# The last expert place of a fused state-space scan and hash-routed MoE kernel: separate PSUM banks, a last product in two pieces, GpSimd's drain moved ahead of six scatters

## Chip, cores, metric

The kernel runs on one core of one Trainium2 chip. The metric is the device time of one execution in microseconds, the median of several runs. TensorE is called PE, VectorE DVE, ScalarE ACT, GpSimd POOL and SyncE SP, as the profile names them.

## What is computed

Two layers, one after the other, all in float32. The first is a chunked state-space scan (Mamba-2 SSD) for 4 batches, 8 heads and 768 positions. Its output is laid out as 3072 tokens of 256 values. The second sends each token to one of 8 experts by its id and applies a two-layer MLP with 256, 1024 and 256 features:

```python
expert_idx = token_ids * np.int64(2654435761) % np.int64(E)
for e in range(E):
    mask = expert_idx == e
    xe = x[mask]
    h = np.maximum(xe @ w1[e], 0.0)
    out[mask] = h @ w2[e]
```

The change lies in the last part of the second layer.

## The kernel before, in words

The kernel first runs the scan and writes its tokens to DRAM, and beside it works out for every token a slot: the tokens of one expert lie next to each other. The experts take 8 "places" p = 0 to 7, sorted by their number of tokens; place p has two halves of `HALF[p]` slots (202 down to 184). `xT` holds the slots' vectors with features on partitions; 25 tiles of 128 slots cover all slots, and the halves' borders don't fall on the tiles' borders. Place 7 has its halves at slots 2816 to 2999 and 3000 to 3183. The tiles 22, 23 and 24 are its own: tile 22 lies in the first half, tile 23 holds the end of the first half and the first 72 slots of the second, and tile 24 the last 112.

Each product of a 2 by 2 block matrix (halves of features by halves of slots) is done with 7 block products in place of 8 (Strassen's scheme in Winograd's form): sums of weight blocks (`sums_w`, on POOL, tiles s1 and s2), sums of operand blocks (`sums_x`, `sums_h`, on DVE, tiles t1 and t2), 7 products on PE and sums of the products on the way out of PSUM. `up` (L898 is its matmul) makes the first layer, `down` (L943) the second. One product of `down` is 4 matmuls of a 128x128 weight block with up to 202 columns; the trace shows each float32 matmul as two, so 8 passes a product.

The products are numbered: `down(p, 1)` leaves p1 (copied by ACT, L950), 6 leaves u2 = product + p1 (DVE, L955), 2 adds to 1 in PSUM and is the block o(0, 0) of the output (ACT, L952), 7 adds to 6 in PSUM and leaves u3 (DVE, L960), 4 adds to the same bank and gives o(1, 0) (DVE, L964), 5 leaves z in PSUM, o(1, 1) = z + u3 (DVE, L966), and 3 adds to z's bank and gives o(0, 1) = bank + u2 (DVE, L962). In o(i, j), i is the half of the features and j the half of the slots. The outputs overwrite `xT`.

`put(k)` turns tile k back (two PE transposes, L970, into one PSUM bank, then one copy to `o_sb`, L975 on ACT or L973 on DVE), and `scatter` sends its 128 rows to their tokens in the output with an indirect DMA that POOL issues (L979). `o_sb` has 4 buffers.

PE, DVE, ACT and POOL run their instructions in the order of the program text (the schedule is written by hand). `step(p)` interleaves `up(p)` with `down(p - 1)`. After `step(7)` only `down(7)` is left, which I call the last place: the sums of place 7's operand (`sums_h`, L872, L875, L877 and L879 in this order), then the products in the order 1, 6, 2, 7, 4, 5, 3, with banks given by `banks=(4, 5, 0)`: 1 and 2 in bank 4, 6, 7 and 4 in bank 5, 5 and 3 in bank 0. The last product of place 6 uses bank 4 too. The tiles of place 6 (19, 20, 21) are put after the products 1, 6 and 2, one each, all through bank 7; then POOL gets a drain instruction (L1111). Tile 22 is put ahead of the last product, the tiles 23 and 24 after it. Behind this stands a loop for experts with more tokens than their slots, which runs zero times with this input, and then the end of the program, where every engine waits for all DMAs and for each other (its instructions stand under L1122 and L1194).

Of the kernel before, what the change touches and what calls it, by code (L numbers as in the profile page):

```python
# [25 lines left out]
def kernel(  # L26
# [900 lines left out]

    dsts = {p: {} for p in range(E)}

    def down(p, what, banks=None):  # L930
        n, st = HALF[p], dsts[p]
        banks = banks or (DN[p % 2], DN[1 - p % 2], DN[p % 2])
        bank = banks[1 if what in (6, 7, 4) else 2 if what in (5, 3) else 0]
        w, s, t = w2s[p], s2[p], t2[p]
        A = lambda i, k: (lambda q: w[:, k * Q4 + q, i * P:(i + 1) * P])
        Sm = lambda i: (lambda q: s[:, i, q])
        hq = lambda k: (lambda q: hx[p][:, k, q, 0:n])
        tt = lambda i: (lambda q: t[:, i, q, 0:n])
        lhs, rhs = {1: (A(0, 0), lambda q: h11[p][:, q, 0:n]), 2: (A(0, 1), hq(1)), 3: (Sm(3), hq(2)),
                    4: (A(1, 1), tt(3)), 5: (Sm(0), tt(0)), 6: (Sm(1), tt(1)), 7: (Sm(2), tt(2))}[what]  # L940
        first = what in (1, 6, 5)
        for q in range(Q4):
            pe.matmul(out=ps[:, bank, 0:n], lhsT=lhs(q), rhs=rhs(q), start=(first and q == 0), stop=True,  # L943
                      skip_group_check=True)
        src = ps[:, bank, 0:n]
        o = lambda i, j: xT[:, i, slots(p, j)]
        dwork = lambda name: mwork.tile([P, N0], F32, name=name, bufs=1)[:, 0:n]
        if what == 1:
            st["p1"] = dwork("dp1")
            act.activation(st["p1"], src, AF.Copy)  # L950
        elif what == 2:
            act.activation(o(0, 0), src, AF.Copy)  # L952
        elif what == 6:
            st["u2"] = dwork("du2")
            dve.tensor_tensor(out=st["u2"], in0=src, in1=st["p1"], op=OP.add)  # L955
        elif what == 5:
            st["z"] = src
        elif what == 7:
            st["u3"] = dwork("du3")
            dve.tensor_tensor(out=st["u3"], in0=src, in1=st["p1"], op=OP.add)  # L960
        elif what == 3:
            dve.tensor_tensor(out=o(0, 1), in0=src, in1=st["u2"], op=OP.add)  # L962
        else:
            dve.tensor_tensor(out=o(1, 0), in0=src, in1=st["p1"], op=OP.add)  # L964
        if what in (5, 7) and "z" in st and "u3" in st:
            dve.tensor_tensor(out=o(1, 1), in0=st["z"], in1=st["u3"], op=OP.add)  # L966

# [66 lines left out]
    def step(p):  # L1034
# [12 lines left out]
        for r in range(R):  # L1047
# [22 lines left out]
                sums_x(*xs_.pop(0))  # L1070
            if p == 1 and r == 4:
                pool_e.tensor_copy(out=space, in_=t2[0][:, 3, 0, 0:1])
            if downs:
                down(p - 1, downs[r])
                if downs[r] == 4 and p + 1 < E:
# [17 lines left out]
        step(p)  # L1093

    puts = [k for k in outs if done_at[k] == E - 2]
    for i in range(4):
        sums_h(E - 1, i)
    own = [k for k in outs if done_at[k] == E - 1]
    half = [k for k in own if (k + 1) * P <= base[E - 1, 1]]
    sent = []  # L1100
    for r, w in enumerate((1, 6, 2, 7, 4, 5, 3)):
        if w == 3:
            sent = [put(k, 1 + i) for i, k in enumerate(half)]
        down(E - 1, w, banks=(4, 5, 0))
        if puts:
            scatter(*put(puts.pop(0)))
        if r == 3:
            for k in puts:
                scatter(*put(k))
            puts = []  # L1110
            pool_e.drain()  # L1111
    for o in sent:
        scatter(*o)
    for i, k in enumerate(k for k in own if k not in half):
        scatter(*put(k, (2, 3)[i % 2], eng=(act, dve)[i % 2]))

    _, rn = nc.values_load_multi_w_load_instructions(
        nov_i[0:1, 0:1], min_val=0, max_val=NCH + E,
# [80 lines left out]
```

## Time and profile before

| | |
|---|---|
| median of 3 runs | 241.43 us (239.32 to 243.09) |
| the profiled execution's own time | 242.91 us |
| its span, first to last instruction | 240.9 us |
| PE busy | 219.1 us (91%), 2264 matmuls |
| DVE busy | 175.7 us (73%) |
| POOL busy | 175.1 us (73%) |
| ACT busy | 92.0 us (38%) |

The span is what the trace covers; the profiled execution takes 2.0 us beyond it. A busy PE is counted with modelled ends of its matmuls, so the spacing from one matmul to the next tells more than the busy time. In a timeline a row gives start, length, engine, line, operation, tiles, and in brackets how long the engine had been idle before and what it waited for.

### The profile page before, as it was taken

Reading aid. Unit: us, or ns where it says so; the run is one execution under the profiler, and the core shown is the slowest. Engines: PE = TensorE matmul, PEld = TensorE weight load, DVE = VectorE, ACT = ScalarE, POOL = GpSimd, SP = SyncE. Lnnn points to the kernel's source line nnn. Section 1 sums busy time; section 2 is a strip of 40 time slices with the busy share of each in tenths; the row PEclk is TensorE's granted clock in tenths of the full one; section 3 lists DMA queues with packets and bytes.
Section 4 is the critical chain, followed back from the end, with each engine's and each line's share of the span. In section 5 each row is a group of like instructions: output and inputs, shape, how many; then the busy total and the mean of one; then the engine's idle time right before and its main releaser. Section 6 shows DMA issues by size and latency. Waiting matters only on the chain.

```text
span 240.9 us, 5848 instructions
## 1 busy us (share of the span) xinstructions
PE 219.1 (91%) x2264; PEld 201.2 (84%) x2264; DVE 175.7 (73%) x309; ACT 92.0 (38%) x192; POOL 175.1 (73%) x223
## 2 busy tenths in 40 slices
PE   7979898997859899999999999999999999999880
PEld 2668776875758699998989999999999899998770
DVE  6888979675614779899998976788678389556520
ACT  5866855934245533113033314234303422411210
POOL 8748599913535368589979988999998998980513
PEclk9999999999979999999999999999999999999995
DMA  7999899994878597019118318407107004310101
GB/s 96 160 198 136 171 187 194 171 263 148 221 179 294 186 324 215 27 51 306 61 44 272 122 44 264 174 23 220 44 0 218 28 23 134 113 61 0 46 22 63
DMA packets 52833, 33.14 MB, mean 138 GB/s; under 512 B 29708, under 2 KB 47140, under 8 KB 52806
## 3 DMA queue, kind: packets, MB, share of 16 engines
q1 hardware_dynamic: 48258, 25.74, 44.5%
q0 software_dynamic: 2400, 6.43, 8.2%
q10 hardware_dynamic: 2148, 0.60, 1.0%
q8 instruction: 18, 0.29, 0.5%
q14 instruction: 9, 0.07, 0.1%
HBM read 26.47 MB, written 6.42 MB: 137 GB/s over the span
## 4 chain that ended last, share of the span: by engine, by line
PE 43%; POOL 18%; DVE 15%; DMA 12%; issue 6%; ACT 4%; another core or an unknown queue 0%; POOLq 0%; DVEq 0%; ACTq 0%
PE ps L898 16%; DMA out_dram<-o_sb,idx_out 12%; POOL s L770 10%; PE ps L943 8%; POOL out_dram L979 4%; PE ps L370 4%; PE ps L311 3%; PE ps L153 3%; POOL xg L623 3%; DVE t L863 2%; DVE m L317 2%; PE ps L383 2%; PE ps L265 2%; DVE t L872 2%; DVE t L875 2%
## 5 line engine op out<-in xcount | busy, mean ns | idle before, releaser
L623 POOL DMA_INDIRECT xg<-y_tokens,idx_in x25 | 28.8, 1151 | 21.7 <-DVE m L317 8.2
L979 POOL DMA_INDIRECT out_dram<-o_sb,idx_out x25 | 28.8, 1151 | 18.7 <-ACT o_sb L975 9.1
L898 PE MATMUL ps<-t,s 128*128 128x202 f32 (+7 forms) x192 | 37.3, 329 | 1.2 <-ACT h L908 0.6
L770 POOL TENSOR_TENSOR s<-w 128x512 f32<-128x512 f32 x26 | 33.4, 1284 | 5.1 <-DMA w<-in_moe_w_dram 4.8
L943 PE MATMUL ps<-t,s 128*128 128x202 f32 (+7 forms) x192 | 35.3, 326 | 0.2 <-DVE t L875 0.2
L898 PEld LDWEIGHTS ps<-t,s 128*128 128x128 f32 x192 | 31.3, 189 | 2.5 <-DVE u L913 1.5
L943 PEld LDWEIGHTS ps<-t,s 128*128 128x128 f32 x192 | 31.8, 189 | 0.4 <-issue 0.4
L898 PE MATMUL ps<-xT,w 128*128 128x202 f32 (+7 forms) x128 | 26.8, 342 | 4.3 <-ACT p L904 4.1
L898 PEld LDWEIGHTS ps<-xT,w 128*128 128x128 f32 x128 | 21.6, 198 | 5.8 <-ACT p L904 5.0
L926 ACT ACTIVATE hx<-hx 128x404 f32<-128x404 f32 (+7 forms) x16 | 8.2, 524 | 32.9 <-DVE hx L925 32.7
L317 DVE COPY_PREDICATED m<-cmask,ps 128x1024 f32<-128x1024 int32 x12 | 15.2, 1310 | 4.4 <-ACT y_sb L393 3.9
L770 POOL TENSOR_TENSOR s<-w,s 128x512 f32<-128x512 f32 x13 | 17.9, 1380 | 0.5
L770 POOL TENSOR_TENSOR s<-s,w 128x512 f32<-128x512 f32 x13 | 17.8, 1372 | 0.5
L975 ACT ACTIVATE o_sb<-ps 128x256 f32<-128x256 f32 x24 | 9.2, 382 | 19.1 <-PE ps L970 10.2
L370 PEld LDWEIGHTS ps<-x_t,m 128*64 128x64 f32 x384 | 12.3, 138 | 3.9 <-issue 1.7
L370 PE MATMUL ps<-x_t,m 128*64 128x64 f32 x384 | 13.6, 225 | 2.0 <-ACT y_sb L393 0.8
L354 ACT ACTIVATE z<-z,half 128x256 f32<-128x256 f32 x22 | 10.0, 503 | 10.7 <-DVE z L348 8.7
L904 ACT ACTIVATE p<-ps 128x404 f32<-128x404 f32 (+7 forms) x16 | 7.9, 493 | 15.8 <-PE ps L898 12.2
L913 DVE TENSOR_TENSOR u<-ps,p 128x404 f32<-128x404 f32 (+7 forms) x16 | 8.6, 554 | 6.3 <-PE ps L898 4.3
L863 DVE TENSOR_TENSOR t<-xT 128x202 f32<-128x202 f32 (+7 forms) x16 | 12.3, 770 | 1.0 <-ACT xT L637 1.0
L943 PE MATMUL ps<-t,w 128*128 128x202 f32 (+7 forms) x64 | 11.9, 329 | 1.0 <-DVE du L960 1.0
L554 POOL TENSOR_SCALAR laneoh<-iota,lane 128x128 bf16<-128x128 f32 x18 | 12.2, 696 | 0.3 <-DVE stile L543 0.3
(190 smaller groups left out, 484.0 us busy)
## 6 DMA issues: line engine op xcount, KB each, us to landing
w<-in_moe_w_dram SPq DMA_DIRECT2D x16, 512.0 KB, 8.6
w<-in_moe_w_dram SPq DMA_DIRECT2D x8, 1024.0 KB, 10.0
x_t<-in_x_dram SPq DMA_DIRECT2D x12, 256.0 KB, 6.6
y_tokens<-y_sb SPq DMA_DIRECT2D x10, 256.0 KB, 3.9
raw<-in_B_dram SPq DMA_DIRECT2D x12, 128.0 KB, 4.7
raw<-in_C_dram SPq DMA_DIRECT2D x12, 128.0 KB, 3.6
y_tokens<-y_sb ACTq DMA_DIRECT2D x2, 256.0 KB
xg<-y_tokens,idx_in POOLq DMA_INDIRECT x25
```

Of the source, the lines that this page charges most:

```text
L317: dve.copy_predicated(out=m_sb[k % 2][:, g0:g1].rearrange("q g b i -> q g (b i)"), mask=cmask.bitcast(I32).rearrange("q j i -> q (j i)").u ...
L354: act.activation(z4s[un][:, :, j], zs[un].rearrange("q b e d -> q b (e d)"), AF.Copy, scale=half4[:, j:j + 1])
L370: pe.matmul(out=o, lhsT=m_sb[k % 2][:, g, b, e * T:(e + 1) * T], rhs=xs[k][:, b, 2 * g + e], start=first(g // 2 * 2 + b % 2, c), stop=True ...
L554: eng.tensor_scalar(out=laneoh[:, i], in0=iota_n, scalar1=lane[:, i:i + 1], scalar2=None, op0=OP.is_equal)
L623: pool_e.indirect_dma_start(out=xg[k], out_offset=None, in_=y_dram[0:n, :], in_offset=bass.IndirectOffsetOnAxis(ap=idx_in[:, k:k + 1], axi ...
L770: eng.tensor_tensor(out=s[:, i], in0=a_, in1=b_, op=o)
L863: dve.tensor_tensor(out=t[:, i], in0=a_, in1=b_, op=OP.subtract)
L898: pe.matmul(out=ps[:, bank, i * n:(i + 1) * n], lhsT=lhs[:, (q0 + i) * P:(q0 + i + 1) * P], rhs=rhs, start=(first and i == 0), stop=True, ...
L913: dve.tensor_tensor(out=st["u2"], in0=src, in1=st["p1"], op=OP.add)
L943: pe.matmul(out=ps[:, bank, 0:n], lhsT=lhs(q), rhs=rhs(q), start=(first and q == 0), stop=True, skip_group_check=True)
L975: act.activation(o_sb, ps[:, bank, at:at + DM], AF.Copy)
L979: st = pool_e.indirect_dma_start(out=out[:], out_offset=bass.IndirectOffsetOnAxis(ap=idx, axis=0), in_=o_sb, in_offset=None, bounds_check= ...
```

## The change

The last place is written anew. The sum L872 moves ahead of the last product of place 6, so that on DVE it precedes that product's addition. POOL's drain moves to before the last place, ahead of the scatters of tiles 19 to 21. The products get banks of their own: 1 and 2 in bank 5, 6 and 7 in bank 4, 4 in bank 3 by itself (its result is then added to u3 in place of p1), 5 in bank 1. All three tiles of place 6 are put after the first product, through the banks 7, 6 and 0. Tile 22 is put between the two halves of product 5. The last product is cut at the border of the tiles 23 and 24: 72 columns into bank 4 and 112 into bank 5; z is added to u2 beforehand by one more DVE instruction, and each piece gets its own addition. The transposes of the last two tiles are taken apart: those of the features' second half run between the pieces, and each goes to its half of `o_sb` by a copy of 128 columns (tile 23 on ACT, tile 24 on DVE).

```diff
-    def down(p, what, banks=None):
+    def down(p, what, banks=None, alone=False, mid=None):
...
-        first = what in (1, 6, 5)
+        first = what in (1, 6, 5) or alone
         for q in range(Q4):
+            if mid and q == Q4 // 2:
+                mid()
...
-            dve.tensor_tensor(out=o(1, 0), in0=src, in1=st["p1"], op=OP.add)
+            dve.tensor_tensor(out=o(1, 0), in0=src, in1=st["u3" if alone else "p1"], op=OP.add)
...
+            if p == E - 1 and r == R - 1:
+                sums_h(p, 0)
             if downs:
                 down(p - 1, downs[r])
...
-    for i in range(4):
-        sums_h(E - 1, i)
...
-    sent = []
-    for r, w in enumerate((1, 6, 2, 7, 4, 5, 3)):
-        if w == 3:
-            sent = [put(k, 1 + i) for i, k in enumerate(half)]
-        down(E - 1, w, banks=(4, 5, 0))
-        if puts:
-            scatter(*put(puts.pop(0)))
-        if r == 3:
-            for k in puts:
-                scatter(*put(k))
-            puts = []
-            pool_e.drain()
-    for o in sent:
-        scatter(*o)
-    for i, k in enumerate(k for k in own if k not in half):
-        scatter(*put(k, (2, 3)[i % 2], eng=(act, dve)[i % 2]))
+    rest = [k for k in own if k not in half]
+    assert len(rest) == 2 and len(half) <= 2
+    o_own, sent = [], []
+
+    def part(m, i, bank, at, eng):
+        k = rest[m]
+        if i == 1:
+            o_own.append(mwork.tile([P, DM], F32, name="o_sb", bufs=4))
+        pe.transpose(out=ps[:, bank, at:at + P], in_=xT[:, i, k * P:(k + 1) * P], identity=ident)
+        o, src = o_own[m][:, i * P:(i + 1) * P], ps[:, bank, at:at + P]
+        if eng is dve:
+            dve.tensor_copy(out=o, in_=src)
+        else:
+            act.activation(o, src, AF.Copy)
+
+    def put_half():
+        for i, k in enumerate(half):
+            scatter(*put(k, (OB, XB)[i]))
+
+    pool_e.drain()
+    for i in range(1, 4):
+        sums_h(E - 1, i)
+    for w in (1, 6, 2, 7, 4, 5):
+        b = {1: 5, 2: 5, 6: 4, 7: 4, 4: 3, 5: 1}[w]
+        down(E - 1, w, banks=(b,) * 3, alone=w == 4, mid=put_half if w == 5 else None)
+        if w == 1:
+            for i, k in enumerate(puts):
+                sent.append(put(k, (OB, XB, 0)[i]))
+            for o in sent:
+                scatter(*o)
+    n, st, cut = HALF[E - 1], dsts[E - 1], rest[1] * P - base[E - 1, 1]
+    dve.tensor_tensor(out=st["u2"], in0=st["z"], in1=st["u2"], op=OP.add)
+    for m, (c0, c1, bank) in enumerate(((0, cut, 4), (cut, n, 5))):
+        for q in range(Q4):
+            if m == 1 and q == Q4 // 2:
+                part(0, 0, 0, 256, act)
+            pe.matmul(out=ps[:, bank, 0:c1 - c0], lhsT=s2[E - 1][:, 3, q], rhs=hx[E - 1][:, 2, q, c0:c1],
+                      start=(q == 0), stop=True, skip_group_check=True)
+        dve.tensor_tensor(out=xT[:, 0, base[E - 1, 1] + c0:base[E - 1, 1] + c1], in0=ps[:, bank, 0:c1 - c0],
+                          in1=st["u2"][:, c0:c1], op=OP.add)
+        if m == 0:
+            part(0, 1, 0, 0, act)
+            part(1, 1, 2, 0, dve)
+    part(1, 0, 2, 256, dve)
+    for m in range(2):
+        scatter(o_own[m], idx_out[:, rest[m]:rest[m] + 1])
```

Up to L930 the changed kernel has the line numbers of the kernel before; in `down`, `put` and `scatter` its lines stand two to three further down (the matmul of `down` is L945, the sum o(0, 1) L964, the transposes of `put` L972).

In a listing of an engine's order, a row is one instruction (or several alike, "x3"), with what it waits for in brackets; `t_` is the operand sums of `sums_h`, `h_` and `hx` the first layer's output, `w_` and `s_` the weights of the second layer and their sums, `du`, `dp` the tiles u2, u3 and p1 of `down`.

DVE, at the end of `step(7)` and through the last place, before:

```order
L920 TENSOR_TENSOR hx<-ps,u_2418 128x2x184 [waits PE_49]
L920 TENSOR_TENSOR hx<-ps,u_2427 128x2x184 [waits PE_49]
L962 TENSOR_TENSOR xT<-ps,du_2455 128x186 [waits PE_49]
L872 SCALAR_TENSOR_TENSOR t_2514<-hx,h_2440 128x4x184 [waits DVE_49]
L875 TENSOR_TENSOR t_2514<-hx,t_2514 128x4x184 [waits DVE_49,Activation_49]
```

and with the change:

```order
L920 TENSOR_TENSOR hx<-ps,u_2418 128x2x184 [waits PE_49]
L920 TENSOR_TENSOR hx<-ps,u_2427 128x2x184 [waits PE_49]
L872 SCALAR_TENSOR_TENSOR t_2509<-hx,h_2440 128x4x184 [waits DVE_49]
L964 TENSOR_TENSOR xT<-ps,du_2455 128x186 [waits PE_49]
L875 TENSOR_TENSOR t_2509<-hx,t_2509 128x4x184 [waits DVE_49,Activation_49]
```

The sum L872 stands ahead of the addition of place 6's last product (L962, now L964).

PE, the last place from the first put behind product 1 to product 4, before (the first `t_2514` with `s_2399` is product 6, `hx` with `w_2375` product 2, the second `t_2514` with `s_2399` product 7, `t_2514` with `w_2375` product 4):

```order
L970 MATMUL ps<-ident,xT 128x128 x2
L943 MATMUL ps<-t_2514,s_2399 128x184 [waits DVE_49,Pool_49]
L943 MATMUL ps<-t_2514,s_2399 128x184 x3
L970 MATMUL ps<-ident,xT 128x128 [waits Activation_49]
L970 MATMUL ps<-ident,xT 128x128
L943 MATMUL ps<-hx,w_2375 128x184 x4
L970 MATMUL ps<-ident,xT 128x128 [waits Activation_49]
L970 MATMUL ps<-ident,xT 128x128
L943 MATMUL ps<-t_2514,s_2399 128x184 [waits DVE_49]
L943 MATMUL ps<-t_2514,s_2399 128x184 x3
L943 MATMUL ps<-t_2514,w_2375 128x184 [waits DVE_49]
L943 MATMUL ps<-t_2514,w_2375 128x184 x3
```

and with the change:

```order
L972 MATMUL ps<-ident,xT 128x128 x2
L972 MATMUL ps<-ident,xT 128x128 [waits DVE_49]
L972 MATMUL ps<-ident,xT 128x128 x3
L945 MATMUL ps<-t_2509,s_2399 128x184 [waits DVE_49,Pool_49]
L945 MATMUL ps<-t_2509,s_2399 128x184 x3
L945 MATMUL ps<-hx,w_2375 128x184 [waits Activation_49]
L945 MATMUL ps<-hx,w_2375 128x184 x3
L945 MATMUL ps<-t_2509,s_2399 128x184 [waits DVE_49]
L945 MATMUL ps<-t_2509,s_2399 128x184 x3
L945 MATMUL ps<-t_2509,w_2375 128x184 x4
```

The six transposes of place 6's tiles stand together behind product 1, and product 4 has lost its wait for DVE.

PE, from the put of tile 22 to the last transpose (`hx` with `s_2399` is the last product), before:

```order
L970 MATMUL ps<-ident,xT 128x128 [waits Activation_49]
L970 MATMUL ps<-ident,xT 128x128 [waits DVE_49]
L943 MATMUL ps<-hx,s_2399 128x184 [waits DVE_49]
L943 MATMUL ps<-hx,s_2399 128x184 x3
L970 MATMUL ps<-ident,xT 128x128 [waits DVE_49]
L970 MATMUL ps<-ident,xT 128x128 x3
```

and with the change:

```order
L972 MATMUL ps<-ident,xT 128x128 [waits Activation_49]
L972 MATMUL ps<-ident,xT 128x128 [waits DVE_49]
L945 MATMUL ps<-t_2509,s_2399 128x184 x2
L1138 MATMUL ps<-hx,s_2399 128x72 x4
L1110 MATMUL ps<-ident,xT 128x128 [waits DVE_49]
L1110 MATMUL ps<-ident,xT 128x128
L1138 MATMUL ps<-hx,s_2399 128x112 x2
L1110 MATMUL ps<-ident,xT 128x128 [waits DVE_49,Activation_49]
L1138 MATMUL ps<-hx,s_2399 128x112 x2
L1110 MATMUL ps<-ident,xT 128x128 [waits DVE_49]
```

The last product is eight matmuls in place of four, and only one transpose is left behind its end.

## Rows read from the trace of the kernel before

**Rows 1.** The windows view, three stages: length, PE, PEld, DVE, ACT, POOL busy, granted clock.

```profile
221.94:231.95 10.01, 9.13 (x56) 8.33 (x56) 4.77 (x8) 1.77 (x6) 3.03 (x3) 1.00 0.12 41
231.95:236.38 4.43, 2.17 (x12) 1.65 (x12) 0.83 (x3) 0.64 (x2) 1.97 (x2) 0.95 0.08 30
236.38:240.92 4.54, 0.00 (x0) 0.00 (x0) 0.00 (x0) 0.00 (x0) 0.99 (x1) 0.50 0.15 54
```

**Rows 2.** Timeline, all engines: the border of place 6 and the last place.

```profile
219.65 1.17 DVE L920 TENSOR_TENSOR hx<-ps,u 128x368 f32<-128x368 f32 x2 [0.27 <-PE ps L898]
220.07 1.42 PE L943 MATMUL ps<-hx,s 128*128 128x186 f32 x8
221.53 0.35 DVE L962 TENSOR_TENSOR xT<-ps,du 128x186 f32<-128x186 f32 x1 [0.72 <-PE ps L943]
221.80 0.92 DVE L872 SCALAR_TENSOR_TENSOR t<-hx,h 128x736 f32<-128x736 f32 x1
221.94 1.51 PE L943 MATMUL ps<-h,w 128*128 128x184 f32 x8 [0.44 <-DVE xT L962]
222.82 0.93 DVE L875 TENSOR_TENSOR t<-hx,t 128x736 f32<-128x736 f32 x1
223.29 0.38 PE L970 MATMUL ps<-ident,xT 128*128 128x128 f32 x2
```

**Rows 3.** Timeline, all engines: where PE waits within the last place.

```profile
223.89 1.49 PE L943 MATMUL ps<-t,s 128*128 128x184 f32 x8 [0.22 <-DVE t L875]
228.75 1.51 PE L943 MATMUL ps<-t,w 128*128 128x184 f32 x8 [0.44 <-DVE du L960]
231.96 1.51 PE L943 MATMUL ps<-hx,s 128*128 128x184 f32 x8 [0.22 <-DVE xT L966]
```

**Rows 4.** Timeline, all engines: from the last product to the last scatter.

```profile
233.51 0.35 DVE L962 TENSOR_TENSOR xT<-ps,du 128x184 f32<-128x184 f32 x1 [1.61 <-PE ps L943]
233.57 0.98 POOL L979 DMA_INDIRECT out_dram<-o_sb,idx_out  x1 [4.78 <-issue]
233.91 0.66 PE L970 MATMUL ps<-ident,xT 128*128 128x128 f32 x4 [0.44 <-DVE xT L962]
234.44 0.39 ACT L975 ACTIVATE o_sb<-ps 128x256 f32<-128x256 f32 x1 [2.23 <-PE ps L970]
234.66 0.42 DVE L973 COPY o_sb<-ps 128x256 f32<-128x256 f32 x1 [0.80 <-PE ps L970]
235.09 0.98 POOL L979 DMA_INDIRECT out_dram<-o_sb,idx_out  x1 [0.54 <-ACT o_sb L975]
236.38 0.99 POOL L979 DMA_INDIRECT out_dram<-o_sb,idx_out  x1 [0.30 <-issue]
```

**Rows 5.** Timeline: short instructions on PE, DVE and ACT, for the new sizes.

```profile
9.10 0.81 PE L218 MATMUL ps<-usel,tot 128*128 128x16 f32 x6 [0.30 <-ACT fac L247]
...
206.74 0.54 DVE L913 TENSOR_TENSOR u<-ps,p 128x368 f32<-128x368 f32 x1 [0.81 <-PE ps L898]
...
223.54 0.32 ACT L950 ACTIVATE dp<-ps 128x184 f32<-128x184 f32 x1 [4.69 <-PE ps L943]
```

**Rows 6.** Lines' view, sequencer instructions: count, duration ns min/median/max, first and last start.

```profile
L1111 POOLq DRAIN  x1: 5139/5139/5139, 227.6 to 227.6; - x1
L1194 POOLq DRAIN  x3: 51/103/302, 239.7 to 240.6; - x3
L1194 PEldq DRAIN  x2: 8/8/8, 240.0 to 240.3; - x2
```

**Rows 7.** Timeline of POOL: its last sum, and a scatter ahead of the drain.

```profile
217.20 0.19 POOL L772 COPY space<-s 128x1 f32<-128x1 f32 x1
224.41 1.04 POOL L979 DMA_INDIRECT out_dram<-o_sb,idx_out  x1 [7.03 <-ACT o_sb L975]
```

**Rows 8.** The page's groups: the 50 indirect DMAs of POOL.

```profile
L623 POOL DMA_INDIRECT xg<-y_tokens,idx_in x25 | 28.8, 1151 | 21.7 <-DVE m L317 8.2
L979 POOL DMA_INDIRECT out_dram<-o_sb,idx_out x25 | 28.8, 1151 | 18.7 <-ACT o_sb L975 9.1
```

## Prediction, made before the changed kernel was run

> **What bounds the kernel now.** I read the windows first, then the timeline around the border between place 6 and the last place, then the timeline up to the last scatter, then POOL's sequencer rows. Up to the last place PE never rests and the change leaves it alone, so only the last 19 us count: from the last product of place 6 (220.07) to the end (240.92). The windows cut them into three stages [rows 1]: seven products and four puts in 10.01 us, a tail of 4.43 us from the start of the last product to the start of the last scatter, and 4.54 us from there to the end, in which no compute engine works but POOL: that is the scatter's landing and the end of the program. The third stage hangs on the start of the last scatter alone. So the question is how much earlier than 236.38 that scatter starts.
>
> In the first stage PE is short of work four times, each time waiting for DVE. Product 1 waits for DVE's addition of place 6's last product, which uses the same bank: it starts at 221.94, where 221.33 was possible [rows 2]. Product 6 waits for the sum L875, product 4 for DVE's read of product 7's bank, the last product for DVE's read of product 5's bank [rows 3]. In the second stage the chain is single file [rows 4]: product, addition (233.51 to 233.86), four transposes, a copy by ACT (to 234.83), scatter at 235.09, and the last scatter 1.29 later, which is 0.98 of POOL's time plus 0.30 between two scatters. DVE's copy is done at 235.08, so the last scatter waits for POOL, not for its data.
>
> **The change, part by part.** All times are those of the profiled execution: 242.91 us, 2.0 more than its span, and 1.48 above the median of the three runs, so the sum is a difference that I take from both.
>
> The pace of PE: eight passes of 184 columns took 1.51 us after a wait [rows 3], and of 186 columns 1.42 without one [rows 2]; the last pass overhangs, and the next product can start 0.155 x 8 = 1.24 after the one before (221.94 to the put at 223.29 is 1.35, of which 0.10 is the first pass after a wait [rows 2]). A pair of transposes takes 0.38, of which 0.27 is the overhang of the last, so 0.11 each [rows 2].
>
> Start of the last place: place 6's last product starts at 220.07 and has 186 columns, 1.26 [rows 2]. With product 1 in bank 5 nothing holds it: 221.33. L872 now precedes the addition on DVE: the two L920 end at 220.82, so L872 runs 220.92 to 221.83, the addition until about 222.10, L875 until 222.94 (durations 0.92, 0.35 and 0.93 [rows 2]). The three puts, 6 x 0.11 = 0.65, run after product 1 from 222.57; the second needs the addition, done by then. Product 6 can start at 223.22, and L875 is done: cover 0.28, a thin one; if L875 came 0.3 later, product 6 would come about 0.1 later. From here on each product's bank is free and each sum is done one product earlier: 6 (223.22), 2 (224.47), 7 (225.71), 4 (226.96, own bank, no wait), 5 (228.20). The put of tile 22 in its middle costs 0.22; it needs DVE's o(1, 0), done at 228.36 + 0.04 + 0.35 = 228.75, just ahead of PE, which comes to the second transpose at 228.93. The last product starts at 229.66 where it started at 231.96 [rows 3]. That is 2.30 earlier, and it is what stood there as waits; the work (six products, four puts) is the same.
>
> The last product in two pieces: there is no row with 72 or 112 columns over a full 128x128 float32 block, but there are rows on both sides: 16 columns took 0.81 for six passes, less 0.26 for the last one, 0.11 a pass [rows 5], and 128 columns 0.11 [rows 2]. So I take 0.11 for both, 0.86 for each piece, and 0.48 more for the two than for one product. The Trainium skill ("TensorE: Matmul & The Clock Gate", Back-to-back issue gap) gives N / 2.4 + 2.5 ns for one matmul, 33 and 49 ns here, by which the two pieces would take an estimated 0.65 and the sum would come out some 0.8 lower, at 238.0; the rows speak against it, since 184 columns would take 79 ns by it and took 155.
>
> After the cut the chain is: piece 0 from 229.66, its last pass ends near 230.65; two transposes of the other features 230.52 to 230.74; first half of piece 1 to 231.17; the transpose of tile 23's last quarter, which needs the addition of piece 0 (72 columns: from 0.54 for 368 and 0.35 for 184 columns [rows 4, 5] some 0.23, done at 230.93) and ACT's first copy (128 columns: some 0.28, from 0.39 for 256 and 0.32 for 184 [rows 4, 5], done at 231.14). It ends at 231.52, ACT copies until 231.87, and POOL starts the first of the two scatters 0.27 later, as at 234.83 and 235.09: 232.14. The second half of piece 1 ends at 231.95, its addition at 232.27, transpose 232.65, DVE's copy 233.03 (128 columns: 0.29 by the slope). That data would be ready for POOL at 233.29, but POOL is free only 1.29 after 232.14: 233.43. So the last scatter starts 236.38 - 233.43 = 2.95 earlier; what is late next is POOL's spacing of two scatters, by 0.14. The additional DVE instruction (z added to u2, 0.35) runs while PE does piece 0 and costs nothing; without that cover it would delay piece 0's addition by at most 0.35.
>
> POOL: the drain took 5.14 us from 227.6 [rows 6] and let the scatter of tile 22 start at 233.57, 1.4 after its data, which cost the end nothing, as POOL was free at 234.55 and the next scatter was due at 235.09 [rows 4]. Now it stands behind POOL's last sum, 217.39 [rows 7]. With 5.14 it ends at 222.5, some 0.8 later POOL goes on, and the first of the three scatters has its data at about 223.4. They need 3 x 1.29 and are through by 227.6; tile 22's comes at 229.95. The drain could last 4 us more without harm. The queue behind it on POOL holds the six scatters only; ACT's first copies into their buffers wait for older scatters and not for these. But three more scatters now follow the last drain, and the program ends with another drain. That one took 0.30 after 3 scatters, and the long one 5.14 after 47 of the 50 indirect DMAs [rows 6, 8]: 0.10 and 0.11 for each. If it is paid by the DMA, the last drain takes 0.60, and as PE is through at 240.01 beside its end at 240.0 [rows 6], 0.30 comes on top of the end. The bounds: nothing, if the last drain has a fixed time; or, if the three scatters issued right before it made the long one long, 1.71 each, 5.1 in all. I take 0.30, the value to which both rows point.
>
> Sum: -2.30 in the first stage, -0.65 in the second, +0.30 in the third: -2.65. The profiled execution would take 240.3; from the median, 241.43 - 2.65 = 238.8.
>
> **Rivals.** (a) PE's waits come back in the new places: each of the four transposes that run between products has only 0.02 to 0.28 of cover, and a wait costs its length and 0.10 for the next first pass. Five such places at 0.2 to 0.3 take 1.2 of the gain: 240.0. For it: the transpose of tile 23's last quarter is due at 231.17 and its last input at 231.14. Against: the other inputs are done a product earlier. (b) A piece costs by its columns: 184 columns at 0.155 are 0.84 ns a column, so 0.06 and 0.09 a pass. Piece 0 would save 0.37 and the first half of piece 1 0.05, and both scatters come 0.4 earlier: 238.4. Against it stands the row of 16 columns. The formula of the Trainium skill named above points this way too. (c) Slower: the last drain is priced by the scatters since the drain before it, at more than 0.98 each; from there it eats the whole 2.95. At its upper bound of 1.71 the end comes 5.1 - 2.95 = 2.2 later: 243.6. Against it: the last drain had three scatters behind it too and took 0.30. (d) The waits are not those of the banks: PE's brackets name DVE's instructions, and the new order still waits for DVE at products 6 and 7. If only the tail shrinks and product 1's wait goes, the gain is 0.61 + 0.65 - 0.30 = 0.96: 240.5.
>
> **How the numbers follow.** Forecast 0.73, (a) 0.12, (b) 0.07, (c) 0.03, (d) 0.05. The mechanism alone gives 238.2 to 240.0. The three runs lie 2.1 below and 1.7 above their median, and a new median can miss by about half to the whole of it, which widens the range to 236.4 to 240.9; (c) is left out. Two per cent, about what a measurement of this kernel can tell from no change, are 4.8 us; the forecast is 1.1%. Faster by more than that takes 2.2 us of luck beside the forecast: 0.10. Slower by over 2% needs (c) and a bad run: 0.02. Within 2%: 0.88.
>
> **What would show it.** Product 1 of the last place at 1.26 after place 6's last product, and no bracket with a wait for DVE at products 1, 6 and 4. The last product's first pass 9.6 us after the start of place 6's last product. Passes of 72 and 112 columns 0.11 apart. The two last scatters 1.29 apart and the last one 13.4 after place 6's last product, where it was 16.3. A drain of about 5 us in front of the last place, and POOL's last drain of 0.6. It would be wrong if a wait of PE for ACT or DVE over 0.3 stood between the pieces, if the scatters of place 6's tiles started later than 226, or if more than 5 us lay between the last scatter's start and the end.

## The result, and the profile after it

| | before | changed |
|---|---|---|
| median of 20 runs each | 241.3 us (238.99 to 244.34) | 239.03 us (235.64 to 243.79) |
| ratio of the times | | 0.9877, 95% interval 0.9841 to 0.9914 |
| the profiled execution's own time | 242.91 us | 237.17 us |
| its span | 240.9 us | 235.3 us |
| start of place 6's last product | 220.07 | 217.21 |
| from there to the end | 20.85 us | 18.13 us |

The changed kernel is 1.2% faster by that ratio, within 2%, as forecast, and its median lies in the forecast's range (238.8 us, 236.4 to 240.9). The ratio and its interval compare only runs in the faster of two states that executions of this kernel show (11 of the 20 changed ones), so it differs from the ratio of the medians over all runs, 0.991. The two profiled executions differ by 2.4%, and the table's last two rows say why: of the 5.6 us between the spans, 2.86 lie ahead of place 6's last product, in work that the change leaves alone. The start of that product lay between 216.5 and 224.4 us over the profiles of all kernels below, the changed kernel alone giving 217.21 and 224.37 in two profiles. So in the experiments times are counted from that start, and I call the rest of the program the stage; the prediction's three stages are its parts. These two profiles gave 18.13 and 18.14 us for it.

The windows view of the changed kernel, in the three stages of [rows 1] (the first one taken from place 6's last product; length, then PE, PEld, DVE, ACT, POOL busy, granted clock):

```profile
217.21:226.84 9.63, 9.63 (x67) 9.60 (x66) 5.40 (x10) 1.86 (x6) 3.69 (x3) 1.00 0.13 42
226.84:230.57 3.73, 2.62 (x21) 2.20 (x20) 1.70 (x6) 0.56 (x3) 1.96 (x2) 1.00 0.10 35
230.57:235.35 4.78, 0.00 (x0) 0.00 (x0) 0.06 (x1) 0.00 (x0) 0.98 (x1) 0.76 0.15 51
```

The same three windows of before are 11.89, 4.42 and 4.54 us long. In the first PE is now busy for 9.63 of 9.63 us: no wait is left. The second is 0.69 shorter, with more work in it (21 matmuls for 12). The third is 0.24 longer; no engine but POOL works in it, apart from one short DVE instruction of 0.06 us.

Where PE waited before [rows 2, 3], the timeline of the changed kernel shows:

```profile
217.21 1.42 PE L945 MATMUL ps<-hx,s 128*128 128x186 f32 x8
217.99 0.93 DVE L872 SCALAR_TENSOR_TENSOR t<-hx,h 128x736 f32<-128x736 f32 x1
218.47 1.41 PE L945 MATMUL ps<-h,w 128*128 128x184 f32 x8
218.83 0.34 DVE L964 TENSOR_TENSOR xT<-ps,du 128x186 f32<-128x186 f32 x1
219.09 0.92 DVE L875 TENSOR_TENSOR t<-hx,t 128x736 f32<-128x736 f32 x1
219.72 0.82 PE L972 MATMUL ps<-ident,xT 128*128 128x128 f32 x6
220.37 1.41 PE L945 MATMUL ps<-t,s 128*128 128x184 f32 x8
...
224.12 1.41 PE L945 MATMUL ps<-t,w 128*128 128x184 f32 x8
```

No PE row has a bracket. Product 1 starts 1.26 behind place 6's last product, product 6 at 3.16, and the sum L875 that it needs ends at 220.01, 0.36 ahead of it.

The tail, to set beside [rows 4]:

```profile
226.84 1.00 PE L1138 MATMUL ps<-hx,s 128*128 128x72 f32 x8
227.12 0.98 POOL L981 DMA_INDIRECT out_dram<-o_sb,idx_out  x1 [1.98 <-ACT o_sb L977]
227.68 0.38 PE L1110 MATMUL ps<-ident,xT 128*128 128x128 f32 x2
227.88 0.23 DVE L1140 TENSOR_TENSOR xT<-ps,du 128x72 f32<-128x72 f32 x1 [0.24 <-PE ps L1138]
228.03 0.28 ACT L1115 ACTIVATE o_sb<-ps 128x128 f32<-128x128 f32 x1 [1.19 <-PE ps L1110]
228.37 0.33 PE L1110 MATMUL ps<-ident,xT 128*128 128x128 f32 x1
228.73 0.28 ACT L1115 ACTIVATE o_sb<-ps 128x128 f32<-128x128 f32 x1 [0.42 <-PE ps L1110]
229.28 0.98 POOL L981 DMA_INDIRECT out_dram<-o_sb,idx_out  x1 [1.19 <-ACT o_sb L1115]
229.56 0.33 PE L1110 MATMUL ps<-ident,xT 128*128 128x128 f32 x1 [0.44 <-DVE xT L1140]
229.93 0.29 DVE L1113 COPY o_sb<-ps 128x128 f32<-128x128 f32 x1 [0.42 <-PE ps L1110]
230.57 0.98 POOL L981 DMA_INDIRECT out_dram<-o_sb,idx_out  x1 [0.30 <-DVE o_sb L1113]
```

Eight passes of 72 columns fill 226.84 to 227.68, 0.105 each. The only wait of PE that has a bracket is the one for the last addition, in front of the last transpose. The last scatter comes 1.29 behind the one before it, though its own data was ready: DVE's copy ends at 230.22, and 0.27 later is 230.49.

POOL's drains, from the views of their two lines (count, duration in ns min/median/max, first and last start), beside [rows 6]:

```profile
L1121 POOLq DRAIN  x1: 3896/3896/3896, 213.3 to 213.3; - x1
L1226 POOLq DRAIN  x3: 51/103/547, 233.9 to 235.0; - x3
```

The moved drain took 3.9 us and ended 3.6 before POOL's next work. The last one grew from 0.302 to 0.547, and that is the third stage's 0.24.

### The profile page after: what moved, and what is told of

Read it like the earlier page. It is cut to its first block, busy times and chain, and to the rows that moved or that the text cites. A ratio compares the mean times of both kernels' runs of the same rounds, so it can differ in the third digit from the quotient of the medians.

```text
span 235.3 us, 5872 instructions
## 1 busy us (share of the span) xinstructions
PE 217.1 (92%) x2272; PEld 201.3 (86%) x2272; DVE 177.3 (75%) x312; ACT 92.0 (39%) x193; POOL 174.2 (74%) x223
## 4 chain that ended last, share of the span: by engine, by line
PE 68%; DVE 16%; DMA 5%; issue 4%; ACT 3%; SPq 1%; ACTq 0%; POOL 0%; DVEq 0%; POOLq 0%
PE ps L945 25%; PE ps L898 25%; PE ps L370 4%; DMA w<-in_moe_w_dram 4%; PE ps L311 3%; DVE m L317 2%; DVE t L863 2%; PE ps L972 2%; DVE t L872 2%; DMA a_t<-in_a_dram 2%; DVE t L875 2%; PE ps L383 1%; PE ps L631 1%; PE ps L329 1%; PE ps L265 1%
## 5 line engine op out<-in xcount | busy, mean ns | idle before, releaser
L981 POOL DMA_INDIRECT out_dram<-o_sb,idx_out x25 | 27.2, 1090 | 15.7 <-ACT o_sb L977 9.5
L945 PE MATMUL ps<-t,s 128*128 128x202 f32 (+7 forms) x192 | 35.4, 326 | 0.0
L945 PEld LDWEIGHTS ps<-t,s 128*128 128x128 f32 x192 | 31.8, 189 | 0.0
L898 PE MATMUL ps<-xT,w 128*128 128x202 f32 (+7 forms) x128 | 25.8, 331 | 2.8 <-DMA w<-in_moe_w_dram 2.5
L898 PEld LDWEIGHTS ps<-xT,w 128*128 128x128 f32 x128 | 20.6, 190 | 4.4 <-DVE xT L649 3.9
L770 POOL TENSOR_TENSOR s<-s,w 128x512 f32<-128x512 f32 x13 | 17.2, 1324 | 0.5
L370 PEld LDWEIGHTS ps<-x_t,m 128*64 128x64 f32 x384 | 13.5, 151 | 3.1 <-issue 1.1
L370 PE MATMUL ps<-x_t,m 128*64 128x64 f32 x384 | 14.9, 239 | 1.1 <-ACT d_sb L334 0.7
L977 ACT ACTIVATE o_sb<-ps 128x256 f32<-128x256 f32 x23 | 8.6, 383 | 11.6 <-DMA out_dram<-o_sb,idx_out 6.0
L311 PE MATMUL ps<-ce,bt 32*64 32x128 f32 x384 | 11.8, 274 | 0.8 <-DVE key L462 0.7
L945 PE MATMUL ps<-t,w 128*128 128x202 f32 (+7 forms) x64 | 11.8, 327 | 0.5 <-DVE du L962 0.5
```

Source lines behind the costliest of these rows:

```text
L311: pe.matmul(out=ps[u * T:(u + 1) * T, GB + g, b * P:(b + 1) * P].rearrange("q (e i) -> q e i", e=2), lhsT=bts[ck][r, b, c], rhs=ces[ck][r, ...
L370: pe.matmul(out=o, lhsT=m_sb[k % 2][:, g, b, e * T:(e + 1) * T], rhs=xs[k][:, b, 2 * g + e], start=first(g // 2 * 2 + b % 2, c), stop=True ...
L770: eng.tensor_tensor(out=s[:, i], in0=a_, in1=b_, op=o)
L898: pe.matmul(out=ps[:, bank, i * n:(i + 1) * n], lhsT=lhs[:, (q0 + i) * P:(q0 + i + 1) * P], rhs=rhs, start=(first and i == 0), stop=True, ...
L977: act.activation(o_sb, ps[:, bank, at:at + DM], AF.Copy)
L981: st = pool_e.indirect_dma_start(out=out[:], out_offset=bass.IndirectOffsetOnAxis(ap=idx, axis=0), in_=o_sb, in_offset=None, bounds_check= ...
```

## The experiments

The theory is this: the gain comes from PE's four waits, which the banks and the order of the sums take away, and from the shorter tail. The drain must move for these to reach the end, and its price goes by the indirect DMAs since the drain before it. There are two rivals: the drain's move gives most of the gain by itself, or the drain costs nothing wherever it stands.

The stage in numbers, in us: its length, then, counted from its start, the start of the last product, of tile 22's scatter and of the last two scatters, and last the time from the last scatter's start to the end:

| kernel | stage | last product | tile 22's and last two scatters | end behind |
|---|---|---|---|---|
| before | 20.85 | 11.89 | 13.50, 15.03, 16.31 | 4.53 |
| changed | 18.13 | 9.63 | 9.90, 12.07, 13.36 | 4.78 |
| e1, drain alone | 21.09 | 11.89 | 12.41, 15.03, 16.31 | 4.78 |
| e2, drain back | 19.82 | 9.63 | 12.71, 14.00, 15.29 | 4.54 |
| e3, no drain | 21.75 | 9.63 | 9.90, 12.07, 13.36 | 8.38 |
| e4, banks only | 19.83 | 10.30 | 12.71, 14.00, 15.29 | 4.54 |
| e5, uncut | 19.44 | 10.23 | 9.90, 13.37, 14.66 | 4.78 |
| e6, sum late | 18.87 | 10.36 | 10.64, 12.80, 14.09 | 4.78 |
| e7, two drains | 17.88 | 9.63 | 10.51, 12.07, 13.35 | 4.53 |
| e8, turned product | 18.31 | 9.62 | 9.85, 12.23, 13.52 | 4.79 |
| e9, turned, two drains | 17.64 | 9.62 | 10.37, 11.82, 13.11 | 4.53 |

**The drain's move alone (e1).** The kernel before, with

```diff
     sent = []
+    pool_e.drain()
     for r, w in enumerate((1, 6, 2, 7, 4, 5, 3)):
...
             puts = []
-            pool_e.drain()
```

> The kernel before, with the drain alone moved ahead of the last place. Theory (PE's waits for DVE and the tail's single file set the last scatter; a drain of POOL costs about 0.083 us for each indirect DMA since the drain before it): the first drain about 3.7 to 3.9 us, tile 22's scatter 1.1 us earlier, but the last scatter still 16.3 us after the start of place 6's last product; the last drain 0.30 -> 0.55 us and the stage behind the last scatter 4.54 -> 4.73. From place 6's last product to the end 21.0 us where it was 20.85: no gain. Rival (the drain's new place is what brings the gain, since POOL was held up): last scatter at 15.2 us or earlier, 19.8 us in all.

Measured: 21.09, ratio 1.003 (0.9973 to 1.0087). POOL's last scatters in the timeline:

```profile
234.28 0.98 POOL L979 DMA_INDIRECT out_dram<-o_sb,idx_out  x1 [3.69 <-ACT o_sb L975]
236.90 0.98 POOL L979 DMA_INDIRECT out_dram<-o_sb,idx_out  x1 [1.64 <-ACT o_sb L975]
238.18 0.98 POOL L979 DMA_INDIRECT out_dram<-o_sb,idx_out  x1 [0.30 <-issue]
```

Tile 22's scatter comes 1.09 earlier (12.41 for 13.50), the last two not at all, and the end is 0.24 later. So in the kernel before the drain held up nothing that the end waited for, and moving it costs a little: the first rival falls.

**All but the drain's move (e2).** The changed kernel, with

```diff
-    pool_e.drain()
...
             for o in sent:
                 scatter(*o)
+            pool_e.drain()
```

> The changed kernel, with the drain back behind the three scatters of place 6's tiles. Theory: the third of them ends 7.9 us after the start of place 6's last product, the drain then takes 47 x 0.083 = 3.9 us more, and POOL goes on 0.8 later, at 12.6 us, where tile 22's scatter should have come at 9.9: the three scatters left follow each 1.29 apart, the last at 15.2 us in place of 13.4; the last drain 0.30 us, the end 4.5 behind the last scatter; 19.8 us from place 6's last product to the end, 1.7 more than the changed kernel's 18.09. Rival (the drain is hidden wherever it stands): 13.4 and 17.9 us.

Measured: 19.82, ratio 0.9945 (0.9878 to 1.0012). The view of the drain's line, and the last three scatters in the timeline:

```profile
L1131 POOLq DRAIN  x1: 7252/7252/7252, 223.7 to 223.7; - x1
231.84 0.98 POOL L981 DMA_INDIRECT out_dram<-o_sb,idx_out  x1 [4.78 <-ACT o_sb L1115]
233.13 0.98 POOL L981 DMA_INDIRECT out_dram<-o_sb,idx_out  x1 [0.31 <-issue]
234.42 0.99 POOL L981 DMA_INDIRECT out_dram<-o_sb,idx_out  x1 [0.30 <-DMA out_dram<-o_sb,idx_out]
```

The drain counts 7.25 us from its issue, the three scatters among them, and ends 3.92 behind the third one (226.08 + 0.98 = 227.06 to 230.98). All three scatters of the last place then stand in line behind it at 1.29 each. The bracket at 231.84 names ACT's copy L1115, but the last such copy had ended at 230.93, and elsewhere a scatter follows its copy by 0.27. Here POOL went on 0.86 behind the drain's end, as in the kernel before (232.71 to 233.57), so it was the drain that POOL waited for. The second rival falls, and the 1.69 us between 19.82 and 18.13 are what the drain's move is worth once the rest is done. Alone it was worth -0.24 (e1).

**No drain at all (e3).** The changed kernel without the drain's line.

> The changed kernel without any drain of its own. Theory (0.083 us for each indirect DMA since the drain before): last scatter unchanged at 13.4 us after the start of place 6's last product, but the drain at the program's end takes 50 x 0.083 + 0.05 = 4.2 us in place of 0.55, and the end comes 8.3 us behind the last scatter: 21.7 us in all where the changed kernel took 18.09, and slower than the kernel before (20.85). Rival (a drain is long only for scatters issued right before it, or has a fixed time): the last drain 0.55 or less, 18.1 us in all.

Measured: 21.75, ratio 1.0004 (0.9932 to 1.0077): the whole gain is gone. The three drains at the end:

```profile
L1225 POOLq DRAIN  x3: 45/103/4157, 238.9 to 243.6; - x3
```

All scatters start as in the changed kernel, so the drain inside the program changes nothing but the end: without it the end's own drain takes 4.157 us in place of 0.547.

**Banks and order without the cut and without the drain's move (e4).** The kernel before, with

```diff
-        down(E - 1, w, banks=(4, 5, 0))
+        b = {1: 5, 2: 5, 6: 4, 7: 4, 4: 3, 5: 1, 3: 1}[w]
+        down(E - 1, w, banks=(b,) * 3, alone=w == 4)
```

and L872 ahead of place 6's last addition. The puts of place 6's tiles stay one behind each product; tiles 22, 23 and 24 go through the banks 7, 2 and 0.

> The kernel before with the banks of the changed one (and product 4 by itself, L872 ahead of place 6's last addition), but one put after each product, the drain where it was and the last product uncut. Theory: product 1 starts 1.26 us after place 6's last product (was 1.87), product 6 waits some 0.2 for L875, no wait at product 4; z and the last product share a bank, so 0.3 of wait stays there: last product at 10.1 us (was 11.89). The tail alone would put the last scatter at 14.5; but the drain behind the third scatter now ends at about 11.5 and tile 22's scatter comes at 12.3, so the two last ones follow at 13.6 and 14.9. End 4.54 later: 19.4 us where it was 20.85. Rival (the waits come back elsewhere): 20.5 us or more.

Measured: 19.83, ratio 0.9937 (0.9874 to 1.0). The last product starts 1.59 earlier, and the end comes 1.02 earlier, 0.4 less than expected. From the timeline:

```profile
229.92 0.66 PE L970 MATMUL ps<-ident,xT 128*128 128x128 f32 x4 [0.44 <-DVE xT L962]
230.38 0.98 POOL L979 DMA_INDIRECT out_dram<-o_sb,idx_out  x1 [4.78 <-issue]
230.68 0.42 DVE L973 COPY o_sb<-ps 128x256 f32<-128x256 f32 x1 [0.81 <-PE ps L970]
231.67 0.99 POOL L979 DMA_INDIRECT out_dram<-o_sb,idx_out  x1 [0.30 <-DVEq L1125]
```

The drain now lets tile 22's scatter go only at 230.38 (12.71), and the next ones follow at 1.29 each, though both tiles were copied by 231.10. e2, which has the cut and the gathered puts besides, ends within 0.01 of it: with the drain behind the three scatters, these two edits are worth nothing.

**The last product whole (e5).** The changed kernel, with

```diff
-    n, st, cut = HALF[E - 1], dsts[E - 1], rest[1] * P - base[E - 1, 1]
...
-    for m in range(2):
-        scatter(o_own[m], idx_out[:, rest[m]:rest[m] + 1])
+    down(E - 1, 3, banks=(1, 1, 1))
+    for i, k in enumerate(rest):
+        scatter(*put(k, (2, 0)[i], eng=(act, dve)[i]))
```

> The changed kernel with its last product uncut, in z's bank, and the four transposes and two whole copies behind it as before. Theory: PE waits 0.3 us for DVE's read of z, last product at 9.95 us after the start of place 6's last product; tail as before the change, 4.42: last scatter at 14.4 us, end 4.73 later: 19.1 us, 1.0 more than the changed kernel's 18.09. Rival (the cut gains nothing, since its passes cost as much as the transposes it takes out of the tail): 18.1 to 18.4 us.

Measured: 19.44, ratio 0.9928 (0.9887 to 0.9969); one of the ten runs took 770.09 us, is not in the ratio, and nothing here explains it. The cut is worth 1.31 us, 0.3 more than expected, since the whole product, in z's bank, starts 0.60 later than the pieces do, where a wait of 0.3 was expected:

```profile
229.06 1.51 PE L945 MATMUL ps<-hx,s 128*128 128x184 f32 x8 [0.44 <-DVE xT L968]
...
231.02 0.66 PE L972 MATMUL ps<-ident,xT 128*128 128x128 f32 x4 [0.44 <-DVE xT L964]
```

Of the 1.31, 0.60 is the start of the last product (10.23 for 9.63) and 0.71 the time behind it.

**The sum L872 late again (e6).** The changed kernel with `sums_h(p, 0)` back behind the last product of place 6.

> The changed kernel with L872 back behind the addition of place 6's last product. Theory: L875 ends 3.7 us after the start of place 6's last product in place of 2.8, product 6 starts at 3.9 in place of 3.16, and all that follows moves with it: last scatter at 14.1 us, 18.8 us from place 6's last product to the end. Rival (cover further on takes it up): 18.1 us.

Measured: 18.87, one run of 237.17 us without an interval. In the timeline:

```profile
220.09 0.92 DVE L877 SCALAR_TENSOR_TENSOR t<-hx 128x736 f32<-128x736 f32 x1
220.13 1.75 POOL L981 DMA_INDIRECT out_dram<-o_sb,idx_out  x1 [6.29 <-ACT o_sb L977]
220.32 1.49 PE L945 MATMUL ps<-t,s 128*128 128x184 f32 x8 [0.50 <-DVE t L875]
```

Product 6 waits 0.50 for L875, and with the slower first pass and the gap behind it all that follows is 0.73 later. So the one line that moves a sum by one instruction carries 0.73 of the 2.72 us between 20.85 and 18.13. Product 1 still starts at 1.26 here and product 4 has no bracket, so the waits at these two are taken away by the banks and not by the order of the sums.

**A second drain behind the three scatters (e7).** The changed kernel, with

```diff
             for o in sent:
                 scatter(*o)
+            pool_e.drain()
```

> The changed kernel with a second drain behind the three scatters of place 6's tiles. Theory (0.083 us for each indirect DMA since the drain before): the second drain is through 0.3 us after the third scatter, POOL goes on 0.8 later, at 9.0 us after the start of place 6's last product, before tile 22's scatter is due at 9.9; the last drain takes 0.30 in place of 0.55 and the end comes 4.54 behind the last scatter in place of 4.73: 17.9 us in place of 18.09. Rival (a drain has a long fixed time, as the 3.9 us of the first suggests): tile 22's scatter at 12.6 us, the last one at 15.2, 19.8 us in all.

Measured: 17.88, one run of 236.43 us without an interval. The views of the two drains' lines and two scatters:

```profile
L1132 POOLq DRAIN  x1: 5043/5043/5043, 221.4 to 221.4; - x1
L1227 POOLq DRAIN  x3: 51/103/292, 233.4 to 234.3; - x3
...
223.68 0.98 POOL L981 DMA_INDIRECT out_dram<-o_sb,idx_out  x1 [0.30 <-issue]
227.25 0.98 POOL L981 DMA_INDIRECT out_dram<-o_sb,idx_out  x1 [2.59 <-ACT o_sb L977]
```

The last drain is back at 0.292 and the 0.25 at the end are gone. But the second drain ended at 226.40, 1.73 behind the end of the third scatter, where the price by the DMA said 0.3. It pushes tile 22's scatter from 9.90 to 10.51, which costs nothing here, as POOL is free again at 11.8 and the next scatter is due at 12.07.

**The last product turned (e8).** The slots stand on the partitions, the operand is the stationary block and the weights move, and what is added goes into the same bank by a matmul with the identity, so that no transpose is left behind the last product. For tile 23 a POOL instruction ahead of the drain writes zeros and an ACT copy puts 72 columns behind them, which the lines below leave out:

```diff
+    for q in range(Q4):
+        mm(ps[:, 4, 0:P], hpad[:, q, 0:P], s2[E - 1][:, 3, q], q == 0)
+    mm(ps[:, 4, 0:P], xT[:, 0, ks[0]], ident, False)
+    copy(act, 0, 0, ps[:, 4, 0:P])
...
+    mm(ps[:, 5, 0:P], xT[:, 0, ks[1]], ident, True)
+    for q in range(Q4):
+        mm(ps[0:n - cut, 5, 0:P], hx[E - 1][:, 2, q, cut:n], s2[E - 1][:, 3, q], False)
+    copy(act, 1, 0, ps[:, 5, 0:P])
```

> The changed kernel with the last product turned: the operand (112 columns, and 128 with 56 zeros in front for tile 23) is the stationary block and the weight sums the moving one, so the product comes out with slots on partitions; z + u2 goes into xT and is added in PSUM through the identity. No addition by DVE and no transpose is left behind the last product. Theory: both tiles have their data by 12.6 us after the start of place 6's last product, first of the two scatters at 11.6, and POOL's spacing of 1.29 sets the last: 12.9 us where the changed kernel took 13.36, 17.6 us in all. Rival (the identity's passes and the copies take it back): 18.1 us.

Measured: 18.31, ratio 0.988 (0.9774 to 0.9986): a miss. In the timeline:

```profile
231.82 0.28 ACT L1131 ACTIVATE o_sb<-ps 128x128 f32<-128x128 f32 x1 [1.48 <-PE ps L1129]
231.94 0.49 DVE L1130 COPY o_sb<-ps 128x128 f32<-128x128 f32 x2 [0.74 <-issue]
233.00 0.98 POOL L981 DMA_INDIRECT out_dram<-o_sb,idx_out  x1 [1.40 <-DVEq L1152]
```

Tile 23 was copied by two engines. ACT's half was done at 232.10 and DVE's, the first of the two copies in its row, at 232.23; yet the scatter starts at 233.00, 0.77 later and not 0.27. The trace's records of POOL's sequencer show where the time went: POOL's wait for DVE ends at 232.27, and its next record, a move, starts 0.51 later, at 232.78. The same 0.51 stands behind the drain in the kernel before (232.84 to 233.35). What POOL does in it no record shows. Behind a wait for ACT's copy alone, as in the changed kernel, the move starts 0.04 behind the copy (229.01 to 229.05). So the copy by a second engine seems to put this step between the data and the scatter, and e9, where ACT alone copies tile 23, does not have it. The first of the two scatters came 0.6 later than expected by this, and the last one with it.

**The turned product with one copy for tile 23, and two drains (e9).** e8, with

```diff
+            pool_e.drain()
...
+    pe.transpose(out=ps[:, 4, P:DM], in_=xT[:, 1, ks[0]], identity=ident)
+    act.activation(o_own[0], ps[:, 4, 0:DM], AF.Copy)
...
-    copy(act, 1, 0, ps[:, 5, 0:P])
+    dve.tensor_copy(out=o_own[1][:, 0:P], in_=ps[:, 5, 0:P])
```

> The changed kernel with its last product turned (the slots on the partitions, the matrix kept and the weights moving, the sum added by an identity), tile 23's two quarters copied by one ScalarE copy and tile 24's by VectorE, and a second drain of GpSimd behind the first three of the last six scatters. Theory: the first of the last two scatters then waits for one ScalarE copy alone and starts 11.8 us behind the start of the sixth place's last product (12.07 in the changed kernel, 12.23 in the run with the turned product and four copies), the last scatter 1.29 later at 13.1, the last drain takes 0.30 instead of 0.547 and the program ends 4.54 behind that scatter's start: 17.6 us instead of 18.13. Rival: the identity's passes or the wider copy take back what the transposes gave, the last scatter starts at 13.4 or later, and only the drain's 0.25 is gained: 17.9 or more. The difference of the two in the time is 0.2 per cent of it, which the runs' interval will not part; the stage in the profile does.

Measured: 17.64, median of 6 runs 238.16 us, ratio 0.9839 (0.9792 to 0.9886). The tail in the timeline:

```profile
230.28 0.38 ACT L1136 ACTIVATE o_sb<-ps 128x256 f32<-128x256 f32 x1 [1.59 <-PE ps L1135]
230.93 0.98 POOL L981 DMA_INDIRECT out_dram<-o_sb,idx_out  x1 [0.47 <-ACT o_sb L1136]
231.50 0.29 DVE L1142 COPY o_sb<-ps 128x128 f32<-128x128 f32 x1 [0.82 <-PEq L1151]
232.22 0.98 POOL L981 DMA_INDIRECT out_dram<-o_sb,idx_out  x1 [0.30 <-issue]
```

With one engine's copy the scatter follows by 0.27, as expected. This is the shortest stage of all, 0.5 us below the changed kernel, and 0.25 of that is the drain. The interval of its ratio overlaps that of the changed kernel run beside it (after_again). So the runs show that it beats the kernel before; that it beats the changed one is shown by the stage in the profile alone.

**The changed kernel once more (after_again).**

> The changed kernel once more, beside new runs of the kernel before. Theory: the stage from the sixth place's last product to the end takes 18.1 us again, with the last scatter at 13.36, whatever the place at which that product starts (which varied by several us over the runs so far), and the time is 0.988 of the time before with an interval of about a half per cent to each side. Rival: the gain of the first comparison was the spread of the runs ahead of that stage, and the ratio comes out near 1.0.

Measured: 239.41 us, ratio 0.9883 (0.9829 to 0.9936), stage 18.14, last scatter 13.36. The gain is no chance of one set of runs.

## Why the prediction was right

**The place and the sum.** I said that only what lies between place 6's last product and the start of the last scatter counts. The sum was -2.30 - 0.65 + 0.30 = -2.65; the windows give -2.26 - 0.69 + 0.24 = -2.71 (2.72 from the stage's two lengths, by rounding). The medians differ by 2.3 us, and the ratio makes it 2.97 of 241.3 with an interval of 2.1 to 3.8, which holds the sum and the windows' figure. The runs alone could not tell the three terms apart; the windows do.

**First stage.** The steps came nearly as worked out: product 1 at 1.26, product 6 at 3.16 (3.15 said), the last product at 9.63 (9.59 said). L875 was done with 0.36 to spare where I said 0.28. e6 shows that this thin cover is real: one instruction later on DVE costs 0.73. In e6 L875 ends at 3.68 where it ended at 2.80; 0.88 less the 0.36 of cover and with the 0.10 of a first pass is 0.62 by my step, so the step was a little low. The runs split the 2.26: the banks with the earlier L872 give 1.59 (e4, last product at 10.30), gathering the puts 0.07 more (e5, 10.23), and the pieces' own banks the other 0.60 (9.63).

**Second stage.** A pass of 72 columns costs 0.105 us, as the 0.11 of 128: the choice of 0.11 from the rows of 16 and 128 columns held, and rival (b) fell with the formula behind it. The first of the two last scatters came at 12.07, the last at 13.36, both as computed. That they agree to the hundredth is luck: the last product started 0.04 later than I said and the way from there to the scatter was 0.04 shorter. Behind the start of the last product the cut gives 0.71 (e5), where I said 0.65; the other 0.60 of its 1.31 is a wait that the whole product would bring back, which my sum counts in the first stage.

**Third stage.** The price by the DMA held, and its size was a little high: +0.24 where I said +0.30. The misreading is in the long drain. Its 5.14 us [rows 6] count from its issue at 227.6, while the third scatter ran until 228.80; behind that scatter it took 3.92, which is 0.083 for each of 47 DMAs and not 0.11. So the moved drain took 3.9 us where I said about 5, and that cost nothing, as POOL had 3.6 us to spare there. e3 shows the other side of it: without the drain the end pays 4.157. The bound of 1.71 a scatter, and with it rival (c), is out: three scatters added 0.245, 0.082 each.

**The drain's cover.** I costed the drain in its old place at nothing for the kernel before, which e1 confirms. What the prediction did not price is what it would cost if it stayed: 1.69 (e2). My sum has the drain's move only as a cost at the end, but without the move 1.69 of the 2.72 would not have reached the end.

**Rivals (a) and (d)** fall with the first stage: PE has no wait in it, and one of 0.44 in the tail, where the forecast had it. The transpose that (a) named did start late, but by some 0.05 only: ACT's copy before it ended at 228.31 and it started at 228.37.

## What to carry to other kernels

Before you shorten the work of the engine that bounds, look at what the helper engines do in their slack. Here the drain's move is worth -0.24 alone, and the banks, the order of the sums and the cut together are worth 1.03 without it, but all of them 2.72. In this kernel the price of a GpSimd drain grew with each indirect DMA, so it pays to place one where POOL is idle, before the end of the program and not at it. When a change touches one stage of a long program, measure that stage from a fixed instruction: it repeated within 0.01 us in the two profiles of the changed kernel, while its runs spread from 235.64 to 243.79 us.

## What the hardware showed that I had not expected

**The drain has a price by the DMA.** Counted from the end of POOL's instruction before it, the one ahead of the last place took 3.70 us (POOL's copy L772 ends at 213.51 in the changed kernel, the drain at 217.20) with 44 indirect DMAs since the program's start; 3.92 with 47 (before, e2 and e4); 4.157 with 50 (e3); 0.547 with 6 and 0.302 with 3 at the end. One line goes through all of them within 0.05 us: 0.083 us for each DMA and 0.05 besides. Two drains do not fit: those of e7 and e9 had only three scatters since the drain before and ended 1.73 and 1.58 us behind the third one's end, where the line gives 0.3. The trace's DMA records have that third scatter landed at 226.23 in e7 and 228.46 in e9, and the drains end 0.17 and 0.16 later (226.40 and 228.62). That a drain also waits for the landing is argued from these two, not shown.

**A scatter slowed by a sum.** The first of the three scatters took 1.70 us in place of about 1.0. The timeline of the changed kernel, then that of the kernel before is in [rows 7]:

```profile
220.76 0.92 DVE L879 TENSOR_TENSOR t<-hx,t 128x736 f32<-128x736 f32 x1
220.84 1.70 POOL L981 DMA_INDIRECT out_dram<-o_sb,idx_out  x1 [7.33 <-ACT o_sb L977]
```

It began 0.08 behind the start of a DVE sum of two SBUF operands and ended 0.86 behind that sum's end (221.68). In e6 it began 0.04 behind the start of the sum L877, took 1.75, and ended 0.87 behind that sum's end. In the kernel before it took 1.04, and there too a sum was running, but near its end:

```profile
223.66 0.92 DVE L877 SCALAR_TENSOR_TENSOR t<-hx 128x736 f32<-128x736 f32 x1
224.50 0.92 DVE L879 TENSOR_TENSOR t<-hx,t 128x736 f32<-128x736 f32 x1
```

The scatter began at 224.41, when L877 had 0.17 to go, and ended at 225.45, again 0.87 behind that sum's end. The sum L879, which began 0.09 behind the scatter, did not hold it up. This is no peculiarity of the last place: in the twelve traces 90 scatters began while one of the four sums ran, and 85 of them ended 0.86 to 0.89 behind the sum's end. The other five began less than 0.04 behind the sum's start and took 1.00 to 1.01. The Trainium skill ("SBUF — State Buffer", Who interferes with whom) says that a VectorE instruction with two SBUF inputs contends with a GpSimd instruction that reads SBUF, and that the issue order decides who blocks; these rows agree, if the scatter's POOL instruction is one that reads SBUF, which no run here shows by itself. Here the delay cost nothing, since POOL had time to spare until tile 22's scatter.
